# Later rectifications in the expert layers, and a re-timed first cosine layer

## The chip, the cores and the metric

The kernel runs on one core of one Trainium2 chip. The metric is the device time of the whole program in microseconds (us). The engines are TensorE (PE in the rows: matmuls; PEld: its weight loads), VectorE (DVE), ScalarE (ACT), GpSimd (POOL) and SyncE (SP, which only issues transfers). Each engine works through its own instructions in order. A wait of its oldest instruction holds up all that stand behind it.

## The reference, cut to what matters

Three stages follow each other on 1536 tokens of width 512:

```
x = attention(q, k, v)            # 2 x 8 heads, 768 positions, sinks and a window of 128
P = sinkhorn(exp(x @ w_gate))     # weights of 8 experts for each token, 8 rounds
x = sum over e of P[:, e] * (max(x @ w1[e], 0) @ w2[e])     # w1[e] 512x1024, w2[e] 1024x512
h = x @ w_in                      # 512 -> 2048
out = (h * cos(h)) @ w_out        # 2048 -> 512
```

## The kernel before, in words

**Layers.** The kernel treats the eight experts and the two halves of the last stage as ten equal layers: `e` = 0 to 7 are experts (rectified), `e` = 8 (called `E`) and `e` = 9 are the two halves of `w_in` and `w_out` (cosine). Each layer runs for the two batches `b` = 0 and 1, so there are 20 layer-batches. Each has a first part of 28 products and a second part of six output tiles.

**First part.** Every matrix is kept as a high and a low half-precision piece, and a product is six matmuls with 384 columns (high by low, low by high, high by high, for two blocks). The multiplication by `w1` uses a scheme of seven products in place of eight, so sums of products are needed. In the experts (`g1`, with the order of products in `CHAIN`), some sums are made in the accumulating bank itself: after product 0 the bank is copied out by ScalarE (line 935), and only then may product 4 add to the same bank. Other sums are made by VectorE (line 939). When a sum is complete, `act_relu` (lines 882 to 884) makes the high piece (ScalarE), the rectified value (ScalarE) and the low piece (GpSimd, called the remainder below). In the cosine layers (`g1_sums`) all sums are VectorE's (line 997), and `act_cos` makes g = h cos(h) in steps: line 892 on ScalarE, 895 on VectorE, sine and square on ScalarE (900, 901), 904 on VectorE, and the two pieces on GpSimd (906, 908).

**Second part.** `g2_mm` (line 1034) multiplies the pieces `hh` by `w2`, 24 matmuls of 512 columns for each tile of 128 tokens. In a cosine layer, matmuls of the first three tiles are woven between the products as filling.

**Order.** There is no scheduler: the order on every engine is the order in which the program issues. A clock of ticks sets it. A tick passes after each product, and 24 times in the second part; so a layer-batch has GT + HT_ = 28 + 24 = 52 ticks. `put(t0, every, steps)` hangs steps on later ticks. `late` is a list of steps that `flush` issues at the next tick. What a product's result needs (its copy, its sum) is issued one product later, behind the next product's matmuls, by `settle`.

**Weights.** `w_load` loads the next layer's weights into the one buffer `st`, finds their largest magnitude in four steps (`absmax`, line 167, one reduction of 128x1024 on VectorE each), and makes a power-of-two scale from it (`scales`). The scale needs a small matmul on TensorE (line 149) that waits for VectorE's tile `diag` (line 142). `squares` (line 170) is another way to such a bound: a sum of squares on ScalarE, used in the attention stage. `w2_split` and `w1_split` then make the pieces (ScalarE line 189, VectorE line 190). In the loop over the layers, `t2` and `t1` are the ticks for `w2` and `w1` of the next layer: (load; first magnitude step, distance; first split, distance).

**Operands of the cosine layers.** `x2` prepares the last stage's input: for each batch, six calls of `x_operand` (`xops`, three for each half c of the columns), each with three subtractions on GpSimd (lines 204 to 206, tile `T`), three operations on ScalarE, three on VectorE (line 190, tile `xs`), and one transposing transfer into `XO`. The first product of a batch needs all six.

## Time and profile before

| | us |
|---|---|
| median of 3 runs | 1372.41 (1371.7 to 1373.5) |
| the profiled execution: its time | 1374.77 |
| its span | 1373.1 |
| TensorE busy in the span | 1278.2 (93%) |
| VectorE, ScalarE, GpSimd busy | 890.7, 691.9, 640.6 |

The profiled execution is one execution, and its own time is 2.36 us above the median. Attention fills the first part up to about 180 us. The expert layers come next, each of them about 119 us long. The first cosine layer runs from 1116 to 1251 us, the second to the end.

### The profile page before, as it was taken

The numbers are of one execution on the slowest core, as the hardware profiler recorded it, in microseconds if no ns is written. First come the engines' busy times: TensorE is split into PE (matmuls) and PEld (weight loads), VectorE is DVE, ScalarE is ACT, GpSimd is POOL, SyncE is SP. The second block draws the span as 40 slices with busy tenths as digits, with TensorE's granted clock in tenths as the row PEclk, the third lists the DMA queues.
The fourth block names the chain that finished last, engine by engine and source line by source line (L and its number), as shares of the span: only waits on it lengthen the run. The fifth ranks groups of instructions, "written<-read, shape, count | busy, mean of one in ns | idle before, by whom it ended". The sixth has DMA issues, their size and how long they took to land.

```text
span 1373.1 us, 19781 instructions
## 1 busy us (share of the span) xinstructions
PE 1278.2 (93%) x7299; PEld 679.5 (49%) x7299; DVE 890.7 (65%) x1853; ACT 691.9 (50%) x1374; POOL 640.6 (47%) x782
## 2 busy tenths in 40 slices
PE   4656899999999999999999999999999898999998
PEld 3533555454555545455554545545455444454554
DVE  8986852766456653845665475475556589687774
ACT  6565754462635345264444616444371656575552
POOL 4555563521524363263426417333641748377643
PEclk8767899999999999999999999999999999999999
DMA  9798653011112310601231050132112232300001
GB/s 247 159 159 194 160 104 92 1 62 62 62 62 76 125 53 10 199 1 62 79 122 62 16 184 1 62 100 100 62 32 87 45 88 54 89 1 1 32 16 46
DMA packets 140689, 108.78 MB, mean 79 GB/s; under 512 B 100144, under 2 KB 115504, under 8 KB 140592
## 3 DMA queue, kind: packets, MB, share of 16 engines
q1 hardware_dynamic: 126512, 77.22, 21.7%
q0 software_dynamic: 7168, 25.17, 6.1%
q10 hardware_dynamic: 6912, 5.13, 1.4%
q8 instruction: 57, 0.93, 0.3%
q14 instruction: 40, 0.33, 0.1%
HBM read 71.84 MB, written 11.53 MB: 61 GB/s over the span
## 4 chain that ended last, share of the span: by engine, by line
PE 60%; ACT 11%; DVE 9%; POOL 5%; issue 2%; DMA 0%; POOLq 0%; DVEq 0%
PE bank L1034 37%; PE bank L966 19%; ACT tmp L883 4%; ACT hh L882 4%; PE bank L983 3%; DVE tmp L939 2%; DVE tmp L997 2%; ACT tmp L935 2%; DVE wm L167 1%; DVE w1o L190 1%; DVE tmp L895 1%; POOL hh L884 1%; DVE xs L190 1%; DVE tmp L904 1%; POOL S L275 1%
## 5 line engine op out<-in xcount | busy, mean ns | idle before, releaser
L1034 PE MATMUL bank<-w2s,hh 128*128 128x512 f16 x2880 | 639.4, 380 | 6.2 <-POOL hh L906 2.4
L966 PE MATMUL bank<-xo,w1o 128*128 128x384 f16 x2688 | 455.2, 328 | 21.5 <-ACT tmp L935 16.0
L1034 PEld LDWEIGHTS <-hh 128*128 128x128 f16 x2880 | 281.1, 98 | 340.6 <-POOL hh L908 4.5
L884 POOL TENSOR_TENSOR hh<-tmp,hh 128x384 f16<-128x384 f32 x256 | 230.3, 918 | 388.1 <-ACT tmp L883 376.0
L966 PEld LDWEIGHTS <-w1o 128*128 128x128 f16 x2688 | 261.3, 98 | 202.1 <-issue 34.1
L935 ACT ACTIVATE tmp<-bank 128x384 f32<-128x384 f32 x192 | 91.5, 484 | 315.6 <-PE bank L966 314.6
L939 DVE TENSOR_TENSOR tmp<-bank,tmp 128x384 f32<-128x384 f32 x192 | 103.3, 554 | 194.2 <-ACT tmp L935 166.7
L882 ACT ACTIVATE hh<-tmp 128x384 f16<-128x384 f32 x192 | 99.6, 519 | 55.1 <-DVE tmp L939 55.0
L983 PE MATMUL bank<-xo,w1o 128*128 128x384 f16 x672 | 119.4, 328 | 2.8 <-DVE tmp L997 1.2
L1098 DVE SCALAR_TENSOR_TENSOR acc<-bank,PS,acc 128x512 f32<-128x512 f32 x84 | 62.6, 746 | 69.9 <-PE bank L1034 69.8
L883 ACT ACTIVATE tmp<-tmp 128x384 f32<-128x384 f32 x192 | 100.4, 523 | 6.1
L983 PEld LDWEIGHTS <-w1o 128*128 128x128 f16 x672 | 65.9, 98 | 54.6 <-issue 7.7
L167 DVE TENSOR_REDUCE wm<-st 128x1 f32<-128x1024 f32 x72 | 86.3, 1209 | 4.9 <-DMA st<-w_in 4.9
L906 POOL TENSOR_SCALAR hh<-tmp 128x384 f16<-128x384 f32 x64 | 45.7, 714 | 90.2 <-DVE tmp L904 87.7
L189 ACT ACTIVATE w1o<-S,s 128x1024 f16<-128x1024 f32 x40 | 45.8, 1146 | 78.0 <-POOL S L276 77.3
L190 DVE SCALAR_TENSOR_TENSOR w1o<-st,s,w1o 128x512 f16<-128x512 f32 x72 | 65.9, 947 | 18.0 <-ACT w1o L189 18.0
L190 DVE SCALAR_TENSOR_TENSOR w1o<-S,s,w1o 128x1024 f16<-128x1024 f32 x40 | 55.7, 1394 | 28.9 <-ACT w1o L189 28.9
L190 DVE SCALAR_TENSOR_TENSOR w2s<-st,s,w2s 128x512 f16<-128x512 f32 x72 | 57.6, 816 | 24.3 <-ACT w2s L189 24.3
L908 POOL TENSOR_TENSOR hh<-tmp,hh 128x384 f16<-128x384 f32 x64 | 68.3, 1068 | 5.3
L997 DVE TENSOR_TENSOR tmp<-bank,tmp 128x384 f32<-128x384 f32 x112 | 59.2, 548 | 9.6 <-ACT tmp L1005 5.2
L189 ACT ACTIVATE w2s<-st,s 128x512 f16<-128x512 f32 x72 | 46.0, 708 | 22.5 <-DVE s L160 22.5
L579 POOL TENSOR_TENSOR parts<-xo,parts 128x512 f16<-128x512 f32 (+1 forms) x38 | 41.0, 1081 | 34.1 <-ACT parts L574 31.8
(185 smaller groups left out, 1301.7 us busy)
## 6 DMA issues: line engine op xcount, KB each, us to landing
st<-in_moe_w_dram SPq DMA_DIRECT2D x56, 512.0 KB, 6.0
f<-in_moe_w_in_dram POOLq DMA_DIRECT2D x16, 512.0 KB, 4.5
f<-in_moe_w_out_dram POOLq DMA_DIRECT2D x16, 512.0 KB, 4.3
w2p<-in_moe_w_dram SPq DMA_DIRECT2D x8, 512.0 KB, 4.3
w_in<-x POOLq DMA_DIRECT2D x16, 256.0 KB, 4.5
w_out<-x POOLq DMA_DIRECT2D x16, 256.0 KB, 4.3
st<-w_out SPq DMA_DIRECT2D x8, 512.0 KB, 5.3
st<-w_in SPq DMA_DIRECT2D x8, 512.0 KB, 7.0
```

The source lines that it names most:

```text
L167: nc.vector.tensor_reduce(out=dst, in_=src, axis=axis, op=ALU.max, apply_absolute_value=True)
L189: nc.scalar.activation(out=hi, in_=src, func=AF.Copy, scale=s)
L190: late.append(lambda: nc.vector.scalar_tensor_tensor(out=lo, in0=src, scalar=s, in1=hi, op0=ALU.mult, op1=ALU.subtract))
L882: nc.scalar.activation(out=hi, in_=src, func=AF.Relu)
L883: nc.scalar.activation(out=dst, in_=src, func=AF.Relu)
L884: nc.gpsimd.tensor_tensor(out=lo, in0=dst, in1=hi, op=ALU.subtract)
L935: nc.scalar.activation(out=t, in_=ps, func=AF.Copy)
L939: nc.vector.tensor_tensor(out=t, in0=ps, in1=t, op=ALU.add)
L966: nc.tensor.matmul(ps, W1O[:, j0 + c, wi, o, kk, :], XO[b][:, kk, o, xi, :], start=(n == 0 and o in (0, 5, 1)), stop=(n == 5), skip_group_ ...
L983: nc.tensor.matmul(ps, W1O[:, j, wi, o, kk, :], XO[b][:, kk, o, xi, :], start=(n == 0), stop=(n == 5))
L997: nc.vector.tensor_tensor(out=t, in0=x, in1=y, op=ALU.add)
L1034: nc.tensor.matmul(ps, HH[:, hi, f, t * 128:(t + 1) * 128], w[:, wi, f, :], start=(f == order[0] and n == 0), stop=(f == order[-1] and n = ...
```

## The change

Four edits. First, in `g1`, `out` no longer calls `act` at once: the call passes through `late` twice, so that it is issued one product later, behind what the next product's `settle` issues. (Products whose result is rectified straight from the bank, product 6, are not delayed.) Second, the six operands of batch 1 of the first cosine layer: three of them (c = 0) are hung on ticks 4, 11 and 18 of that layer's first part, the other three on ticks 37, 41 and 45, in its second part; before, all six were hung on ticks 5 to 27 of the first part. Third, at `e` = 8 the four magnitude steps of the next `w2` become `squares` on ScalarE, 5 ticks apart. Fourth, other ticks for `e` = 7 and `e` = 8.

```diff
@@ g1
             def out(c, name, ps, half, high):
                 t = q.pop((c, name))
                 nc.vector.tensor_tensor(out=t, in0=ps, in1=t, op=ALU.add)
-                act(t, (NJ if high else 0) + j0 + c, half)
+                late.append(lambda: late.append(lambda: act(t, (NJ if high else 0) + j0 + c, half)))
@@ layers
-                put(HT_ + 5 if b else HT_ + 4, 4.5 if b else 7.0, xops)
+                if b:
+                    put(HT_ + 4, 7.0, xops[:3])
+                    put(HT_ + GT + 9, 4.0, xops[3:])
+                else:
+                    put(HT_ + 4, 7.0, xops)
@@ the loop over the layers
-                ld2, ld1 = w_load(e + 1, "w2", None, st), w_load(e + 1, "w1", None, st)
+                junk = W2S[1][:, 0, 0:2].rearrange("p f w -> p (f w)").bitcast(BF16) if e == E else None
+                ld2, ld1 = w_load(e + 1, "w2", None, st, junk), w_load(e + 1, "w1", None, st)
                 t2, t1 = (3, 9, 3.0, 28, 2.25), (GT + HT_ + -16, GT + HT_ + 6, 2.5, GT + HT_ + GT + 0, 1.0)
...
                 if e == E:
-                    t2, t1 = (0, 5, 3.0, 39, 1.25), (GT + HT_ + -3, GT + HT_ + 0, 3.5, GT + HT_ + GT + 10, 0.5)
+                    t2, t1 = (0, 6, 5.0, 41, 1.4), (GT + HT_ + -1, GT + HT_ + 5, 3.0, GT + HT_ + GT + 10, 0.5)
+                if e == E - 1:
+                    t2, t1 = (3, 8, 2.5, 24, 1.25), (35, 43, 2.0, GT + HT_ + GT + 0, 1.0)
```

**On ScalarE, in an expert layer.** From the end of the first half of the products to the copies of the second half, the rows before are these (L935 copies a bank, L882 and L883 rectify; bank_80 and bank_81 are the two accumulating banks):

```order
L882 ACTIVATE hh<-bank_81 128x384
L883 ACTIVATE tmp<-bank_81 128x384
L882 ACTIVATE hh<-tmp 128x384
L883 ACTIVATE tmp<-tmp 128x384
L882 ACTIVATE hh<-tmp 128x384
L883 ACTIVATE tmp<-tmp 128x384
L882 ACTIVATE hh<-tmp 128x384
L883 ACTIVATE tmp<-tmp 128x384
L935 ACTIVATE tmp<-bank_80 128x384
L935 ACTIVATE tmp<-bank_81 128x384
```

The same place of the same layer now:

```order
L882 ACTIVATE hh<-bank_81 128x384
L883 ACTIVATE tmp<-bank_81 128x384
L882 ACTIVATE hh<-tmp 128x384
L883 ACTIVATE tmp<-tmp 128x384
L882 ACTIVATE hh<-tmp 128x384
L883 ACTIVATE tmp<-tmp 128x384
L935 ACTIVATE tmp<-bank_80 128x384
L882 ACTIVATE hh<-tmp 128x384
L883 ACTIVATE tmp<-tmp 128x384
L935 ACTIVATE tmp<-bank_81 128x384
```

The copy of bank_80 has passed one pair of rectifying operations. The same happens to the copy of bank_81 earlier in each half, which passes the pair of the sum before it. Expert 0's first batch, which is woven into the attention, keeps its order.

**On VectorE, at the start of the first cosine layer.** Before (L997 sums products, L895 and L904 belong to the cosine, L167 is a magnitude step, L190 on `xs` an operand of batch 1):

```order
L997 TENSOR_TENSOR tmp<-bank_80,tmp 128x384
L167 TENSOR_REDUCE wm<-st 128x1
L997 TENSOR_TENSOR tmp<-bank_81,tmp 128x384 x2
L190 SCALAR_TENSOR_TENSOR xs<-acc_75,s,xs 128x2x128
L190 SCALAR_TENSOR_TENSOR xs<-acc_75,s,xs 128x128
L904 SCALAR_TENSOR_TENSOR tmp<-tmp 128x384
L895 SCALAR_TENSOR_TENSOR tmp<-tmp,scl 128x384
L997 TENSOR_TENSOR tmp<-bank_84,tmp 128x384
L895 SCALAR_TENSOR_TENSOR tmp<-tmp,scl 128x384
L190 SCALAR_TENSOR_TENSOR xs<-T,s,xs 128x4x128
L167 TENSOR_REDUCE wm<-st 128x1
```

Now (line 997 has become 998):

```order
L998 TENSOR_TENSOR tmp<-bank_80,tmp 128x384
L190 SCALAR_TENSOR_TENSOR xs<-acc_75,s,xs 128x2x128
L190 SCALAR_TENSOR_TENSOR xs<-acc_75,s,xs 128x128
L998 TENSOR_TENSOR tmp<-bank_81,tmp 128x384 x2
L904 SCALAR_TENSOR_TENSOR tmp<-tmp 128x384
L895 SCALAR_TENSOR_TENSOR tmp<-tmp,scl 128x384
L998 TENSOR_TENSOR tmp<-bank_84,tmp 128x384
L190 SCALAR_TENSOR_TENSOR xs<-T,s,xs 128x4x128
L895 SCALAR_TENSOR_TENSOR tmp<-tmp,scl 128x384
```

The four reductions are gone from this part, and of the six operands three are left in it; the other three stand behind the last line 904 of the part, among the pieces of `w2`.

**On TensorE, around the scale of the next `w2`.** Before, its matmul (line 149) stood after product 17 of the 28 of the first cosine layer's batch 0, with more products behind it:

```order
L1034 LDWEIGHTS hh
L1034 MATMUL bank_85<-w2s_72,hh 128x512
L149 LDWEIGHTS one_93
L149 MATMUL bank_80<-diag,one_93 128x128
L983 LDWEIGHTS w1o
L983 MATMUL bank_81<-xo_69,w1o 128x384
```

Now it stands behind the last product of the batch (line 983 has become 984, line 1034 has become 1035):

```order
L984 LDWEIGHTS w1o
L984 MATMUL bank_78<-xo_69,w1o 128x384
L149 LDWEIGHTS one_93
L149 MATMUL bank_79<-diag,one_93 128x128
L1035 LDWEIGHTS hh
L1035 MATMUL bank_83<-w2s_72,hh 128x512
```

What follows it is the filling that is left over, and the second part.

## Rows read from the trace of the kernel before

**Rows 1.** Waits of TensorE from 278 to 1052 us: total us, times, longest
```profile
PE bank L966 <- ACT tmp L935: 8.7, 14, 1.0
PE bank L1034 <- DVE w2s L190: 1.1, 2, 0.6
```

**Rows 2.** Timeline of TensorE: start, us, instructions, idle time before with releaser
```profile
476.73 1.14 PE L966 MATMUL bank<-xo,w1o 128*128 128x384 f16 x6 [0.95 <-ACT tmp L935]
...
1072.69 1.81 PE L966 MATMUL bank<-xo,w1o 128*128 128x384 f16 x6 [3.45 <-ACT tmp L935]
...
1074.40 10.90 PE L966 MATMUL bank<-xo,w1o 128*128 128x384 f16 x60
```

**Rows 3.** Timeline of ScalarE in expert 2, batch 1, ahead of the first wait above
```profile
468.12 0.47 ACT L935 ACTIVATE tmp<-bank 128x384 f32<-128x384 f32 x1
...
475.24 0.51 ACT L882 ACTIVATE hh<-tmp 128x384 f16<-128x384 f32 x1
475.78 0.52 ACT L883 ACTIVATE tmp<-tmp 128x384 f32<-128x384 f32 x1
476.21 0.85 ACT L935 ACTIVATE tmp<-bank 128x384 f32<-128x384 f32 x2
```

**Rows 4.** Timeline of all engines in expert 7, batch 1, ahead of the second wait
```profile
1069.48 1.20 DVE L167 TENSOR_REDUCE wm<-st 128x1 f32<-128x1024 f32 x1
1069.56 0.45 POOL L206 TENSOR_TENSOR T<-acc,T 128x128 f32<-128x128 f32 x1
...
1070.58 0.71 ACT L189 ACTIVATE xs<-T,s 128x512 f16<-128x512 f32 x1
...
1072.17 0.85 ACT L935 ACTIVATE tmp<-bank 128x384 f32<-128x384 f32 x2
```

**Rows 5.** Windows: first cosine layer's batches 0, 1, second's batch 0; busy us, clock
```profile
1116.22:1191.98 75.76, 64.01 (x316) 30.94 (x315) 62.25 (x123) 45.66 (x84) 40.74 (x50) 0.95 0.35 86
1191.98:1250.97 58.99, 58.59 (x314) 30.51 (x313) 46.86 (x81) 37.37 (x67) 40.92 (x47) 1.00 0.03 13
1250.97:1310.48 59.51, 58.71 (x314) 30.45 (x312) 42.10 (x74) 30.79 (x58) 31.17 (x34) 1.00 0.06 23
```

**Rows 6.** Timeline of TensorE in the first cosine layer, batch 0
```profile
1118.02 3.57 PE L983 MATMUL bank<-xo,w1o 128*128 128x384 f16 x21 [1.14 <-DMA xo<-xs]
1122.54 0.22 PE L149 MATMUL bank<-diag,one 128*128 128x128 bf16 x1 [0.95 <-DVE diag L142]
...
1150.99 0.23 PE L149 MATMUL bank<-diag,one 128*128 128x128 bf16 x1 [4.69 <-DVE diag L142]
...
1170.29 0.61 PE L1034 MATMUL bank<-w2s,hh 128*128 128x512 f16 x2 [2.14 <-POOL hh L906]
1171.29 20.85 PE L1034 MATMUL bank<-w2s,hh 128*128 128x512 f16 x88 [0.39 <-POOL hh L908]
```

**Rows 7.** VectorE on `xs`, 1120 to 1176 us: ns min/median/max, and its idle time
```profile
L190 DVE SCALAR_TENSOR_TENSOR xs<-acc,s,xs x12: 345/542/1039, 1127.0 to 1169.8; 128x256 f16<-128x256 f32 x6, 128x128 f16<-128x128 f32 x6
L190 DVE SCALAR_TENSOR_TENSOR xs<-T,s,xs x6: 735/812/1059, 1131.1 to 1173.5; 128x512 f16<-128x512 f32 x6
...
  ACT xs L189: 2.9, 4
```

**Rows 8.** Magnitude steps on VectorE, 1120 to 1176 us: busy us, mean ns
```profile
L167 DVE TENSOR_REDUCE wm<-st 128x1 f32<-128x1024 f32 x4 | 4.8, 1208 | 0.0
```

**Rows 9.** Timeline of ScalarE at the first sine
```profile
1123.61 1.28 ACT L900 ACT_TABLE_LOAD   x1
...
1125.55 0.52 ACT L901 ACTIVATE tmp<-tmp 128x384 f32<-128x384 f32 x1
```

**Rows 10.** Line 170, sums of squares in the attention: ns min/median/max
```profile
L170 ACT ACTIVATE w1o<-tmp x4: 1039/1040/1041, 24.8 to 30.9; 128x1024 bf16<-128x1024 f32 x4
L170 ACT ACTIVATION_READ_ACCUMULATOR w1o<-tmp x4: 185/186/187, 25.7 to 31.9; 128x1 f32 x4
```

**Rows 11.** Transfers of operands, 1116 to 1192 us: us from issue to landing
```profile
xo<-xs SPq DMA_TRANSPOSE x6, 4.0
```

**Rows 12.** ScalarE takes out the fifth of six tiles, first cosine layer, batch 0
```profile
1187.00 0.69 ACT L1101 ACTIVATE acc<-bank,scl 128x512 f32<-128x512 f32 x1 [2.04 <-PE bank L1034]
```

**Rows 13.** Timeline of GpSimd and TensorE at the end of expert 2's first part, batch 1
```profile
485.30 6.29 POOL L884 TENSOR_TENSOR hh<-tmp,hh 128x384 f16<-128x384 f32 x7 [1.17 <-ACT tmp L883]
...
487.51 4.70 PE L1034 MATMUL bank<-w2s,hh 128*128 128x512 f16 x21
```

## The prediction

> **What bounds the kernel now.** I first read TensorE's busy share by stretch, then the list of what TensorE waits for, then its timeline, which puts each wait in its place. TensorE sets the pace: in the long middle of the program it is nearly always in a matmul, so only what it waits for, or what it does slowly, can be won. Between 278 and 1052 us, where the experts 1 to 7 run, its one large group of waits is 14 waits of at most 1.0 us, 8.7 us together, for the copy of a bank on line 935 [rows 1]. They recur at the same product of each layer-batch, the one that adds to bank A0 at the start of the second half of the products: 0.95 us in six of them, as at 476.73, 0.34 to 0.38 in eight. Expert 7's batch 1 has the same wait, but 3.45 us long, and after it the matmuls are slow for a while: six in 1.81 us where 476.73 shows 1.14, and 60 in 10.90 [rows 2].
>
> The second place is the first cosine layer's batch 0. It takes 75.76 us. The three other cosine batches have the same matmuls; the two that the windows show take 58.99 and 59.51 [rows 5]. So some 16.8 us are lost there. In those 75.76 us VectorE is busy for 62.25, in the next batch for 46.86 [rows 5]. The timeline shows where TensorE pays: 1.14 for the operands at the start, 0.95 and 4.69 for VectorE's `diag`, 2.14 and 0.39 for the pieces of h at the end [rows 6], and small ones between, which wait for VectorE's sums. After the last wait 88 matmuls of 512 columns take 20.85 us; at the pace of row 487.51 (4.70 for 21) they would take some 19.1 [rows 6, 13]. The reader is to see one thing in these rows: VectorE is late by several us all through this batch, and TensorE meets that lag wherever it must.
>
> **The later rectification.** Before the wait at 476.73, the copy that TensorE needs starts at 476.21, directly behind a pair of rectifying operations of 0.51 and 0.52 [rows 3]. The order now puts the copy ahead of that pair. That alone is 1.0 us earlier, enough for the 0.95 and for all shorter ones. The earlier copy, too, no longer waits behind a pair that itself waits for VectorE's sum. I take all 14 waits as gone, 8.7, and give back 0.5, because in expert 1 TensorE then reaches the pieces of `w2`, for which it waited 1.1 us already [rows 1], sooner: **8.2 us**, between 6.5 and 8.7. What is late next is the last rectified pieces of the first part. Row 485.30 shows seven remainders of 0.90 in 6.29 us; the last that the first output tile needs is the fourth, done at 488.9, and TensorE, starting at 487.51 with matmuls of some 0.22, reaches it after 21 of them, at 492.0 [rows 13]. That is 3.1 us of cover against a move of about 1.0, so I cost it at nothing; without the cover it would be 1.0 for each layer-batch. The last sum's remainder belongs to the other half of the tokens, three tiles later.
>
> **Expert 7, batch 1.** The wait costs 3.45, the slow matmuls after it 0.67 and, for the 60 in 10.90 against ten products of 1.02 (row 1118.02: 21 matmuls in 3.57), some 0.7: 4.8 together [rows 2, 6]. Two edits act here: the copy passes one pair, and the four reductions of 1.2 on VectorE, one of which starts at 1069.48 in the midst of the delay [rows 4], move into the second part of the batch before. What remains is an operand: ScalarE's operation at 1070.58 needs GpSimd's `T`, done at 1070.0, and still stands ahead of the copies [rows 4]. Without the reductions I let `T` come 1.5 us earlier (nothing would be the low end, half of four times 1.2, or 2.4, the high one). Then 1068.5, plus 0.71, a pair of 1.0 and a copy of 0.47 is 1070.7; TensorE wants it at 1072.69 - 3.45 = 1069.2. So a wait of about 1.5 stays, with 0.5 for the copy after it, and no slow matmuls: 4.8 - 2.0, **2.7 us**, between 1.0 and 4.8.
>
> **The first cosine layer, batch 0.** VectorE loses four reductions, 4.8 us [rows 8], and three of six operands: the first twelve operations have a median of 0.54 and the other six of 0.81, so 2 x 0.54 + 0.81 = 1.9 each and 5.7 for three; half of the 2.9 us idle before them goes too, 1.4 [rows 7]. Three one-column operations are added, taken at some 0.15 each, 0.5 together. In all VectorE is shorter by 4.8 + 5.7 + 1.4 - 0.5 = 11.4. ScalarE gets four sums of squares, 1.04 + 0.19 each, 4.9 us [rows 10], but the three operands leave it; it was busy for 45.66 of 75.76 [rows 5], so I cost this at nothing. Without that cover it is at most 4.9 on the chain through the cosine.
>
> A rule weighed here. The first sine is preceded by a load of tables of 1.28 us, and the square that follows it at 1125.55 has no load of its own [rows 9]. The changed order has no further load either. The Trainium skill ("ScalarE: Activation LUTs", section "Table sets: the hidden batching unit") says that functions of different sets, when alternated, cost a switch of about 2.7 us each time. By that rule alone, four squares among sines would be eight switches, an estimate of 21 us; the row shows that square and sine share a set, and the sum goes by the row.
>
> TensorE cannot win more than the batch lost: the floor is 58.99 plus the waits of 1.14 and 0.95 at the start, whose chain (GpSimd and VectorE finishing the last layer) the change leaves as it is, so 61.1 and a gain of 14.7. If VectorE stays the bound, the gain is its 11.4. The scale's matmul now stands behind the last product, so TensorE meets VectorE's lag once there. I take **11.0**, nearer to VectorE's figure because the batch was VectorE's; low end 7, if the lag at that matmul is still as large as the 4.69 of before and is not covered.
>
> **Costs behind it.** The three late operands end close to batch 1. The last is begun behind the removal of the fourth tile, one tile of 5.2 us (24 matmuls at 0.22) before row 1187.00 [rows 12]; three operations on ScalarE, two pieces of `w2` and VectorE's part take about 4 us, the transfer 4.0 [rows 11], and about 10.4 us are left to TensorE: cover of some 2 us. Every us beyond it is paid by TensorE at the first product. The load of the next `w1` follows the later splits. I set **1.0 us** for all this, 0 to 3.
>
> **Sum.** 8.2 + 2.7 + 11.0 - 1.0 = 20.9. The profiled execution's own time is 1374.77, so it would be 1353.9; it is 2.4 above the median of 1372.41, and against the median the forecast is **1351.5 us**. With the ends of all terms: gains of 28.2 to 11.5, so 1344.2 to 1360.9. A difference of 0.2%, some 2.7 us, is about what a measurement of this kernel can tell from no change.
>
> **Rivals.**
> 1. VectorE's lag stays and is paid at the scale's matmul. For it: TensorE has paid 4.69 at the same kind of matmul. Against: 11.4 us of VectorE's work have left. With a gain of 5 there and 3 of costs behind it, 8.2 + 2.7 + 5 - 3 = 12.9 less: 1359.5. Chance 0.14.
> 2. The batch clears fully: 8.7 + 4.8 + 14.7 = 28.2, 1344.2. For it: batch 1 with four reductions in it has almost no waits (58.59 busy of 58.99 [rows 5]). Against: three operands and the late start of VectorE remain. Chance 0.13.
> 3. The waits for copies only move, to the remainders or to other copies: the 8.2 falls away, 1359.7. Against it stand 3.1 us of cover. Chance 0.08.
> 4. Slower: the rectified pieces come so late that TensorE waits at the start of the second part in all 14 layer-batches of experts 1 to 7. It pays from 3.1 us of delay on, and outweighs the gain from 3.1 + 20.9 / 14 = 4.6 us on; at 5 us it is 14 x 1.9 = 26.6, so 1378. The order moves the pieces by one pair, 1.0. Chance 0.04.
> 5. The added squares bring table loads after all: eight of 1.28 are 10.2 us on ScalarE, 1361.7 if all are paid. Chance 0.01.
> The forecast itself, within 1346 to 1357, has 0.57, and 0.03 is left for a time within 0.2% of before. Faster 0.93, same 0.03, slower 0.04. The range of 1344 to 1361 takes in the first three rivals and both ends of the terms.
>
> **What the new profile would show.** TensorE's waits for line 935 in the experts near zero, and no new ones for the remainders of line 884. In expert 7's batch 1 a wait under 2 us, without slow matmuls behind it. The first cosine layer's batch 0 at about 65 us, the wait for `diag` at its end under 3 us. At the start of batch 1 a wait for `xo` under 1 us. The forecast is wrong if TensorE waits for the operands of batch 1, if VectorE's busy time in batch 0 stays above 55 us, or if copies still reach ScalarE behind work that waits.

## The result, and the profile after

| | before | after |
|---|---|---|
| median, us | 1372.95 (4 runs) | 1355.68 (4 runs, 1354.42 to 1357.88) |
| ratio, 95% interval | | 0.9877 (0.986 to 0.9894) |
| the profiled execution: time, span | 1374.77, 1373.1 | 1356.48, 1354.8 |

The gain is 17.3 us by the medians and 18.3 by the two profiled executions. The forecast was 20.9, and the time lies inside the range. The parts of the sum did not come out as forecast: two errors of opposite sign made the total look better than its working, and that the total came so near is luck in part.

I read the new trace by stage, from the start of one layer-batch on TensorE's timeline to the start of the next. The last stage ends with TensorE's last matmul, 4.0 us before the end of the span in both traces:

| stretch | before | after | forecast of the change |
|---|---|---|---|
| start to expert 1 (attention, expert 0) | 278.70 | 280.53 | none |
| experts 1 to 7 | 837.52 | 821.18 | -10.9 |
| first cosine layer, batch 0 | 75.76 | 69.55 | -11.0 |
| first cosine layer, batch 1 | 58.99 | 61.41 | +1.0 |
| second cosine layer, both batches | 118.05 | 118.06 | none |

The experts gave 16.3 us, half as much again as forecast. The first cosine layer gave 3.8 where I had 10.0. Expert 0 took back 1.6.

**The experts.** The list of TensorE's waits between 280.53 and 1041.31 us, the stretch of [rows 1], has one row left:

```profile
PE bank L1035 <- DVE w2s L190: 0.2, 1, 0.2
```

All 14 waits for line 935 (8.7 us) are gone, and the waits for pieces of `w2`, which I had expected to grow, have nearly gone too. ScalarE's timeline at the place of [rows 3] shows the copy with one pair behind it that stood in front of it before. It starts 14.8 us after the start of the batch in place of 17.2, the copy at 474.27 already waits for TensorE, and TensorE's row (the last one here) runs through without a wait:

```profile
471.34 0.49 ACT L935 ACTIVATE tmp<-bank 128x384 f32<-128x384 f32 x1
471.73 0.51 ACT L882 ACTIVATE hh<-tmp 128x384 f16<-128x384 f32 x1
472.27 0.52 ACT L883 ACTIVATE tmp<-tmp 128x384 f32<-128x384 f32 x1
472.70 0.47 ACT L935 ACTIVATE tmp<-bank 128x384 f32<-128x384 f32 x1
474.27 0.49 ACT L935 ACTIVATE tmp<-bank 128x384 f32<-128x384 f32 x1 [1.09 <-PE bank L967]
...
456.51 17.71 PE L967 MATMUL bank<-xo,w1o 128*128 128x384 f16 x108
```

In expert 7's batch 1 the timeline of TensorE answers to the second and third row of [rows 2]: a wait of 1.38 where 3.45 stood, and 60 matmuls in 9.91 where they took 10.90.

```profile
1059.54 1.14 PE L967 MATMUL bank<-xo,w1o 128*128 128x384 f16 x6 [1.38 <-ACT tmp L935]
1060.88 9.91 PE L967 MATMUL bank<-xo,w1o 128*128 128x384 f16 x60 [0.21 <-ACT tmp L935]
```

The later rectification costs something in one place, expert 0's batch 1, where the gating of the experts shares GpSimd. Eight remainders run there back to back behind a reduction of the gating (line 647). Counted from the start of the batch, that reduction starts at 25.7 us in place of 25.2 and the remainders at 33.5 in place of 32.4, long after ScalarE has done the first of their pieces (26.8 and 25.8). The waits of TensorE for them (214.74 to 280.53 us) are three times as large as before, 2.2 in place of 0.7:

```profile
PE bank L1035 <- POOL hh L884: 2.2, 2, 1.2
```

**The first cosine layer.** The windows that answer to [rows 5] (length; busy us of TensorE, weight loads, VectorE, ScalarE, GpSimd; granted clock):

```profile
1101.71:1171.26 69.55, 62.05 (x315) 31.05 (x314) 58.76 (x121) 49.36 (x92) 38.86 (x50) 0.95 0.32 74
1171.26:1232.67 61.41, 58.82 (x314) 30.34 (x313) 48.78 (x81) 37.54 (x67) 41.00 (x47) 1.00 0.11 35
```

VectorE's busy time fell by only 3.5 in a batch that became 6.2 shorter, and ScalarE's rose by 3.7. TensorE's timeline answers to [rows 6]:

```profile
1103.40 3.57 PE L984 MATMUL bank<-xo,w1o 128*128 128x384 f16 x21 [1.04 <-DMA xo<-xs]
1107.93 0.22 PE L149 MATMUL bank<-diag,one 128*128 128x128 bf16 x1 [0.96 <-DVE diag L142]
...
1118.48 1.14 PE L984 MATMUL bank<-xo,w1o 128*128 128x384 f16 x6 [1.12 <-ACT tmp L1006]
...
1141.53 3.08 PE L984 MATMUL bank<-xo,w1o 128*128 128x384 f16 x12 [2.25 <-ACT tmp L1006]
...
1146.54 0.26 PE L149 MATMUL bank<-diag,one 128*128 128x128 bf16 x1 [1.93 <-DVE diag L142]
1146.60 24.83 PE L1035 MATMUL bank<-w2s,hh 128*128 128x512 f16 x108
...
1197.69 0.23 PE L149 MATMUL bank<-diag,one 128*128 128x128 bf16 x1 [2.52 <-DVE diag L142]
```

The wait for `diag` fell from 4.69 to 1.93 and the waits for the pieces of h at the end went. Two new ones came, 1.12 and 2.25, for ScalarE's copy of a first product (line 1006). The last row is in batch 1 and new as well: the scale of the next `w1` meets a lag of 2.52, where that matmul waited 0.40 before. The operands of batch 1, for which I had set the 1.0, arrive just in time: the last one lands 0.39 us after the start of the batch, behind three matmuls that do not need it.

### The profile page after: what moved, and what is told of

The parts are those of the page before. It is cut to its first block, busy times and chain, and to the rows that moved or that the text cites. A ratio compares the mean times of both kernels' runs of the same rounds, so it can differ in the third digit from the quotient of the medians.

```text
span 1354.8 us, 19792 instructions
## 1 busy us (share of the span) xinstructions
PE 1272.4 (94%) x7299; PEld 679.7 (50%) x7299; DVE 894.3 (66%) x1852; ACT 692.4 (51%) x1382; POOL 641.1 (47%) x782
## 4 chain that ended last, share of the span: by engine, by line
PE 70%; DVE 5%; POOL 5%; issue 3%; ACT 3%; DMA 0%; POOLq 0%; DVEq 0%
PE bank L1035 38%; PE bank L967 28%; PE bank L984 4%; DVE tmp L998 1%; POOL hh L884 1%; POOL S L275 1%; DVE w1o L190 1%; DVE tmp L904 1%; POOL S L274 1%; POOL S L276 1%; DVE tmp L895 1%; ACT tmp L900 1%; POOL S L273 0%; ACT tmp L901 0%; POOL hh L908 0%
## 5 line engine op out<-in xcount | busy, mean ns | idle before, releaser
L935 ACT ACTIVATE tmp<-bank 128x384 f32<-128x384 f32 x192 | 93.4, 487 | 339.8 <-PE bank L967 338.7
L882 ACT ACTIVATE hh<-tmp 128x384 f16<-128x384 f32 x192 | 98.9, 515 | 13.2 <-DVE tmp L939 13.2
L883 ACT ACTIVATE tmp<-tmp 128x384 f32<-128x384 f32 x192 | 100.4, 523 | 6.1
L906 POOL TENSOR_SCALAR hh<-tmp 128x384 f16<-128x384 f32 x64 | 45.9, 717 | 84.0 <-DVE tmp L904 84.0
L167 DVE TENSOR_REDUCE wm<-st 128x1 f32<-128x1024 f32 x68 | 81.5, 1208 | 0.0
L190 DVE SCALAR_TENSOR_TENSOR w1o<-st,s,w1o 128x512 f16<-128x512 f32 x72 | 64.9, 934 | 15.2 <-ACT w1o L189 15.2
L190 DVE SCALAR_TENSOR_TENSOR w1o<-S,s,w1o 128x1024 f16<-128x1024 f32 x40 | 55.2, 1380 | 20.4 <-ACT w1o L189 20.4
L190 DVE SCALAR_TENSOR_TENSOR w2s<-st,s,w2s 128x512 f16<-128x512 f32 x72 | 56.4, 797 | 10.3 <-ACT w2s L189 10.1
```

What stands on the lines that cost most here:

```text
L167: nc.vector.tensor_reduce(out=dst, in_=src, axis=axis, op=ALU.max, apply_absolute_value=True)
L190: late.append(lambda: nc.vector.scalar_tensor_tensor(out=lo, in0=src, scalar=s, in1=hi, op0=ALU.mult, op1=ALU.subtract))
L882: nc.scalar.activation(out=hi, in_=src, func=AF.Relu)
L883: nc.scalar.activation(out=dst, in_=src, func=AF.Relu)
L935: nc.scalar.activation(out=t, in_=ps, func=AF.Copy)
```

## The experiments

The times of one kernel differ by up to 7 us from run to run, and part of that comes from the attention: TensorE's first product of expert 0 stands at 101.50 us in e2's profile and at 106.30 in e1's. From there on the expert stretch repeats well (821.17 to 821.25 in the twelve profiles with the later rectification), so the verdicts go by stages first. The first cosine layer repeats less well: the changed kernel, e2 and e11 have the same instructions in the same order there, and their batch 0 takes 69.55, 68.30 and 69.91, their batch 1 61.41, 62.79 and 62.70. A difference of 1.3 us in one batch is therefore no difference by itself. Expert stretch, first cosine layer's batch 0 and batch 1, second cosine layer, in us. (In e4, e10 and e11 the second cosine layer starts without the wait of 0.4 to 0.5 us for a first copy that the others have.)

| kernel | median | ratio (interval) | experts 1-7 | batch 0 | batch 1 | second |
|---|---|---|---|---|---|---|
| before | 1373 | 1 | 837.52 | 75.76 | 58.99 | 118.05 |
| after | 1355.68 | 0.9877 (0.986-0.9894) | 821.18 | 69.55 | 61.41 | 118.06 |
| e1 late only | 1357.42 | 0.9886 (0.9871-0.9901) | 821.25 | 75.46 | 59.00 | 118.06 |
| e2 no late | 1370.56 | 0.998 (0.9971-0.9989) | 837.49 | 68.30 | 62.79 | 118.06 |
| e3 magnitudes on VectorE | 1356.23 | 0.9875 (0.9862-0.9889) | 821.20 | 69.39 | 62.80 | 118.07 |
| e4 six operands | 1361.00 | 0.9908 (0.9894-0.9921) | 821.19 | 75.79 | 62.85 | 117.53 |
| e5 late and half | 1356.45 | 0.9879 (0.9865-0.9892) | 821.23 | 68.84 | 64.12 | 118.06 |
| e6 w1 places | 1354.81 | 0.9871 (0.9854-0.9888) | 821.18 | 69.73 | 60.83 | 118.06 |
| e7 sine later | 1362.02 | 0.9927 (0.9914-0.9941) | 821.17 | 71.89 | 62.16 | 123.02 |
| e8 all three | 1366.19 | 0.9952 (0.994-0.9965) | 821.25 | 69.25 | 68.01 | 123.27 |
| e9 copy first | 1352.58 | 0.9848 (0.9829-0.9867) | 821.19 | 69.50 | 59.15 | 118.07 |
| e10 scales later | 1361.29 | 0.9914 (0.9897-0.9931) | 821.18 | 72.99 | 67.59 | 116.92 |
| e11 expert 0 as before | 1354.57 | 0.9861 (0.9842-0.988) | 821.19 | 69.91 | 62.70 | 117.40 |
| e12 copy first, scale later | 1351.23 | 0.9843 (0.9825-0.9861) | 821.19 | 68.73 | 59.01 | 118.07 |

**e1: the later rectification alone.** The kernel before, with one edit:

```diff
-                act(t, (NJ if high else 0) + j0 + c, half)
+                late.append(lambda: late.append(lambda: act(t, (NJ if high else 0) + j0 + c, half)))
```

> Kernel before, with only the later rectification. Theory (the later rectification is worth more than the 8.2 us that I gave it, since it clears the 3.45 us wait of expert 7's batch 1 too): the 14 waits on line 935 go (8.7 us), expert 1 gives 1.1, the 3.45 falls below 1.5, expert 0's batch 1 costs 1.5 to 2.2; 10 to 12 us faster than before, some 1361 to 1363, and the first cosine layer's batch 0 stays near 75 us. Rival (the reductions moved out of expert 7 did the rest): the 3.45 stays at 2.5 or more, 7 to 8.5 us faster, 1364.5 to 1366.

More than either expected: 15.8 us by the medians, and 16.27 in experts 1 to 7, the same as the whole change. Expert 7's batch 1 is 60.36 us long, though its four reductions stand where they stood. Its wait is that of the whole change:

```profile
1060.34 1.14 PE L967 MATMUL bank<-xo,w1o 128*128 128x384 f16 x6 [1.39 <-ACT tmp L935]
```

The cosine layers did not move.

**e2: everything but the later rectification.** The edit is e1's, taken out of the changed kernel.

> The changed kernel without the later rectification (the other edits alone). Theory: the 14 waits on line 935 return, 8.7, with expert 1's 1.1 and part of expert 7's, and expert 0's 2.2 goes; 9 to 11 us slower than the changed kernel, 1365 to 1367, with the first cosine layer's batch 0 at 69 to 70 us. Rival (the two parts help each other, the first cosine layer starts cleaner behind the later rectification): that layer's batch 0 is 72 us or more and the time 1368 or more.

2.6 us faster than before, 14.9 slower than the changed kernel. The expert stretch is back at 837.49. The reductions that were moved out of expert 7 give 0.6 there without the later rectification (63.21 for 63.82) and nothing with it. Batch 0 of the first cosine layer is not worse for the missing edit, 68.30, so the rival falls: the two parts do not help each other. The profile shows more, since from the first cosine layer on this kernel has the instructions and the order of the changed one. The scale's matmul starts 44.9 us after the start of the batch, as in the changed kernel (44.8), but the 108 matmuls behind it take 23.47 in place of 24.83, and in batch 1 TensorE then waits 1.25 for the late operands:

```profile
1158.75 0.22 PE L149 MATMUL bank<-diag,one 128*128 128x128 bf16 x1 [1.32 <-DVE diag L142]
1158.81 23.47 PE L1034 MATMUL bank<-w2s,hh 128*128 128x512 f16 x108
...
1184.01 10.40 PE L983 MATMUL bank<-xo,w1o 128*128 128x384 f16 x63 [1.25 <-DMA xo<-xs]
```

The last operand lands 70.1 us after the start of batch 0 here, and 69.9 us in the changed kernel. Its arrival holds both: what batch 0 wins is waited for at the start of batch 1.

**e3 and e4: which of the two edits made batch 0 shorter.** e3 gives the magnitude steps back to VectorE at their new places (its condition never holds), e4 hangs all six operands on the first part again:

```diff
# e3
-                junk = W2S[1][:, 0, 0:2].rearrange("p f w -> p (f w)").bitcast(BF16) if e == E else None
+                junk = W2S[1][:, 0, 0:2].rearrange("p f w -> p (f w)").bitcast(BF16) if e > 99 else None
# e4
-                if b:
-                    put(HT_ + 4, 7.0, xops[:3])
-                    put(HT_ + GT + 9, 4.0, xops[3:])
-                else:
-                    put(HT_ + 4, 7.0, xops)
+                put(HT_ + 5 if b else HT_ + 4, 4.5 if b else 7.0, xops)
```

> The changed kernel with the magnitudes of the next w2 taken on VectorE again (four reductions of 1.2 us, at the new places), nothing else. Theory A (in the first cosine layer's batch 0 ScalarE's squares hold the copies of line 1006): the two waits of 1.12 and 2.25 us for these copies go, VectorE pays part of 4.8; between 2 us faster and 1 us slower than the changed kernel. Theory B (VectorE is still the bound there, as I forecast): 3 to 5 us slower, 1359 to 1361, with the loss at the scale's matmul and at VectorE's sums.

> The changed kernel with all six operands of batch 1 back in the first part of the first cosine layer's batch 0 (places and pace of before). Theory B (VectorE is the bound): VectorE has 7.1 us more to do there and the batch takes 4 to 7 us longer, 1360 to 1363. Theory A (ScalarE is the bound): three operands are some 3 us of ScalarE's work too, so 2 to 4 us longer, 1357.5 to 1360, with longer waits for line 1006. If neither, within 1 us.

With e1 and the changed kernel these two make a square of four (the ticks of the next `w2` differ too between e1 and the others). The windows of batch 0, in order: e1 (six operands, magnitudes on VectorE), e4 (six, on ScalarE), e3 (three, on VectorE); the changed kernel's (three, on ScalarE) stands above.

```profile
1102.51:1177.97 75.46, 63.51 (x315) 30.92 (x314) 62.72 (x123) 45.62 (x84) 40.48 (x50) 0.95 0.35 86
```
```profile
1099.47:1175.26 75.79, 62.79 (x315) 30.94 (x314) 56.86 (x121) 49.52 (x92) 40.18 (x50) 0.95 0.30 70
```
```profile
1098.08:1167.47 69.39, 61.62 (x316) 30.77 (x314) 61.96 (x118) 45.65 (x84) 38.93 (x50) 0.98 0.32 71
```

The batches as a whole hardly tell reductions from squares: 75.46 and 75.79 with six operands, 69.39 and 69.55 with three. The three operands are worth 6.1 and 6.2. But the end of a batch hides something. Behind the scale's matmul TensorE runs 108 matmuls without a wait, and these took 23.47 in e3, 24.83 in the changed kernel and 25.83 in e4:

```profile
1144.11 0.22 PE L149 MATMUL bank<-diag,one 128*128 128x128 bf16 x1 [1.07 <-DVE diag L142]
1144.16 23.47 PE L1035 MATMUL bank<-w2s,hh 128*128 128x512 f16 x108
```
```profile
1149.54 0.26 PE L149 MATMUL bank<-diag,one 128*128 128x128 bf16 x1 [5.40 <-DVE diag L142]
1149.60 25.83 PE L1035 MATMUL bank<-w2s,hh 128*128 128x512 f16 x108
```

So I also read where VectorE ends the last step of the cosine in batch 0 (line 904), how long it was busy until then, and where the scale's matmul starts, in us from the start of the batch:

| kernel: operands in the first part, magnitudes on | last step of line 904 ends | VectorE busy until then | scale's matmul |
|---|---|---|---|
| e1: six, VectorE | 59.18 | 55.25 | (earlier in the order) |
| e4: six, ScalarE | 58.27 | 50.71 | 50.07 |
| e3: three, VectorE | 52.66 | 49.65 | 46.03 |
| changed: three, ScalarE | 51.46 | 45.92 | 44.83 |
| e2: the same here | 51.57 | 46.04 | 44.93 |

The squares take 4.5 and 3.7 us off VectorE, and its last step ends only 0.9 and 1.2 us earlier. The rest has become waits: VectorE's idle time until then, nearly all of it for ScalarE, rises from 3.9 to 7.6 and from 3.0 to 5.5. The three operands, which need both engines, take 5.6 and 4.8 off VectorE and end its last step 6.5 and 6.8 earlier. So VectorE with the reductions is close to being the bound (busy for 94% of the time in e3), and without them the chain through both engines is. My theory B had the direction; it expected 3 to 5 us where 1.2 are found. Theory A had one half: in e3, without squares, the wait of 1.12 for line 1006 is gone, but the later one is there and 2.76 long. Its ScalarE shows why; the copy of 0.47 stands behind a pair of sine and square that waited for VectorE's reduction of the angle (line 895):

```profile
1137.69 0.61 ACT L900 ACTIVATE tmp<-tmp,scl 128x384 f32<-128x384 f32 x1 [0.91 <-DVE tmp L895]
1138.34 0.52 ACT L901 ACTIVATE tmp<-tmp 128x384 f32<-128x384 f32 x1
1138.77 0.47 ACT L1006 ACTIVATE tmp<-bank 128x384 f32<-128x384 f32 x1
1139.14 0.60 ACT L900 ACTIVATE tmp<-tmp,scl 128x384 f32<-128x384 f32 x1
```

**e5 and e6: where batch 1's loss comes from.** e5 is the kernel before with the later rectification and e4's edit the other way round, nothing else. e6 is the changed kernel with one table entry of before:

```diff
# e6
-                    t2, t1 = (0, 6, 5.0, 41, 1.4), (GT + HT_ + -1, GT + HT_ + 5, 3.0, GT + HT_ + GT + 10, 0.5)
+                    t2, t1 = (0, 6, 5.0, 41, 1.4), (GT + HT_ + -3, GT + HT_ + 0, 3.5, GT + HT_ + GT + 10, 0.5)
```

> Kernel before with two of the edits, the later rectification and half of the operands in the next part; magnitudes on VectorE and all places of the w1 and w2 steps as before. Theory (the half of the operands is worth all that the first cosine layer's batch 0 won, and the new places of w1 cost the 2.4 us of its batch 1): batch 0 at 69 to 70 us, batch 1 at 59 to 60, so 1 to 2.5 us faster than the changed kernel, 1353 to 1354.7. Rival (the new places are what lets the late operands through): batch 1 stays at 61 us or more or batch 0 rises above 71, 1356 to 1358.

> The changed kernel with the places of the second cosine layer's w1 steps as before (magnitudes from 0 with pace 3.5 in place of 5 with pace 3.0, loads two ticks earlier). Theory (the scale's matmul stands where VectorE lags by 2.5 us): its wait in batch 1 falls from 2.52 to about 0.4 us, batch 1 from 61.4 to about 59, 1353.3. Rival (the late operands make VectorE lag there whatever the place): a wait of 2 us or more stays, or comes as a wait for operands, and the time is within 1 us of the changed kernel.

In e5 the rival was right: batch 1 takes 64.12, and its first products wait for the late operands, the cost that I had feared:

```profile
1172.13 11.79 PE L984 MATMUL bank<-xo,w1o 128*128 128x384 f16 x63 [2.76 <-DMA xo<-xs]
...
1193.89 0.22 PE L149 MATMUL bank<-diag,one 128*128 128x128 bf16 x1 [1.21 <-DVE diag L142]
```

The landing of the last operand, counted from the start of batch 0, shows what the other edits do for it: 72.1 us in e5, 71.2 in e3, which has the new places and magnitudes on VectorE, and 69.9 to 70.1 with the squares (changed kernel, e2, e11). So the new places and the squares each bring the operands about 1 us forward. e3 waits 1.25 for them, and e2, with the squares, waits 1.25 too because its batch 0 was that much shorter; the changed kernel waits for none because its batch 0 ended later.

At the scale of `w1` in batch 1 two things meet. e4, which has the new places but no late operands, waits 2.55 there, and e3 2.54; e5, with late operands and the places of before, waits 1.21; e1, with neither, 0.40. e6 shortens that wait from 2.52 to 1.45 and batch 1 to 60.83, between its theory (0.4) and its rival (2 or more); its time cannot be told from the changed kernel's.

**e7 and e8: the first edit's idea in the cosine.** The sine and its square go one product later, in the changed kernel (e7) and in e5 (e8):

```diff
-            for d, f in zip((1, 1, 3), (red, sine, fin)):
+            for d, f in zip((1, 2, 3), (red, sine, fin)):
```

> The changed kernel with the sine and its square issued one product later, in all four cosine batches. Theory (a copy of line 1006 stands on ScalarE behind sine and square, and these wait for VectorE's reduction): the waits of 1.12 and 2.25 us go, the first cosine layer's batch 0 falls from 69.5 to 65 to 67 us, 2 to 4 us faster, 1352 to 1353.5. Rival (the pieces of h come a product too late): waits for lines 906 and 908 of about 1 us at the end of each of the four batches, 1357 to 1360.

> The later rectification, half of the operands in the next part, and the sine a product later; magnitudes and places as before. If both theories hold, batch 0 of the first cosine layer at 65 to 67 us and batch 1 at 59 to 60: 1350 to 1352. If only one of them holds, 1353 to 1355; if none, 1357 or more.

A miss, 6.3 us slower than the changed kernel. The largest wait for line 1006 hardly moves (1.99), and the three batches behind batch 0 now end with waits for the pieces of h. In the second cosine layer's first batch, which had none at its end:

```profile
1275.10 1.69 PE L1035 MATMUL bank<-w2s,hh 128*128 128x512 f16 x7 [0.79 <-POOL hh L908]
1277.07 0.60 PE L1035 MATMUL bank<-w2s,hh 128*128 128x512 f16 x2 [0.28 <-POOL hh L906]
1278.24 17.22 PE L1035 MATMUL bank<-w2s,hh 128*128 128x512 f16 x79 [0.57 <-POOL hh L908]
```

The experts had cover for a later rectification and the cosine has none. e8 adds e5's late operands (a wait of 2.74) to that.

**e9: the copy first.** The opposite remedy on the changed kernel: leave the pair, and issue the copy of a first product ahead of it.

```diff
                 settle()
-                pend.append((None, lambda: use(ps)))
+                if o == 0:
+                    use(ps)
+                else:
+                    pend.append((None, lambda: use(ps)))
                 tick()
```

> The changed kernel with the copy of a first product in the cosine layers (line 1006) issued right behind its own product, ahead of the pairs of sine and square that the order set before it. Theory (these copies are held by one pair each, 1.1 us, and by what the pair waits for): the waits of 1.12 and 2.25 us shrink to nothing and to 1 us or less, the first cosine layer's batch 0 goes from 69.5 to 66.5 to 68 us, 1353 to 1354.5. Rival (VectorE's lag is only met a few us later): the wait at the scale's matmul grows by as much, and the time stays within 1 us.

Both were right, one in each batch. In batch 0 the waits for line 1006 shrink to 0.21, and the wait at the scale grows from 1.93 to 4.14: the scale's matmul starts 44.5 us after the start of the batch in place of 44.8, so VectorE's lag is met a few us later, and the batch stays at 69.50. In batch 1 the wait of 2.52 at the scale is gone and the batch is back at 59.15. TensorE's timeline in batch 0 (the edit has moved line 1006 to 1009, 998 to 1001):

```profile
1137.49 1.14 PE L984 MATMUL bank<-xo,w1o 128*128 128x384 f16 x6 [0.21 <-ACT tmp L1009]
1138.99 1.14 PE L984 MATMUL bank<-xo,w1o 128*128 128x384 f16 x6 [0.37 <-DVE tmp L1001]
1144.27 0.22 PE L149 MATMUL bank<-diag,one 128*128 128x128 bf16 x1 [4.14 <-DVE diag L142]
```

**e10: the scales later.** The changed kernel with its magnitude steps spread wider, so that scale and matmul come later:

```diff
-                    t2, t1 = (0, 6, 5.0, 41, 1.4), (GT + HT_ + -1, GT + HT_ + 5, 3.0, GT + HT_ + GT + 10, 0.5)
+                    t2, t1 = (0, 6, 7.0, 41, 1.4), (GT + HT_ + -1, GT + HT_ + 6, 6.0, GT + HT_ + GT + 10, 0.5)
```

> The changed kernel with the magnitudes of the second cosine layer's weights spread wider, so that both scales' matmuls stand 7 and 13 ticks later, behind the last product, where TensorE needs nothing of VectorE. Theory (1.93 and 2.52 us are paid only because the matmul of line 149 stands where VectorE lags): both waits fall under 0.5, batch 1 back to 59 us, batch 0 to 67 to 68; 3 to 4.5 us faster, 1351 to 1352.7. Rival (the lag stays and is met at the pieces of h): new waits for lines 906 and 908 and less than 1.5 us won.

A miss: the waits are 3.88 and 6.26, longer than before the move. VectorE's timeline ahead of the first shows the reason. The steps of the scale now stand behind further steps of the cosine (line 904), and the last of these wait for ScalarE:

```profile
1147.16 0.56 DVE L904 SCALAR_TENSOR_TENSOR tmp<-tmp 128x384 f32<-128x384 f32 x1 [0.44 <-ACT tmp L901]
1148.22 0.68 DVE L904 SCALAR_TENSOR_TENSOR tmp<-tmp 128x384 f32<-128x384 f32 x1 [0.50 <-ACT tmp L901]
1148.82 0.14 DVE L253 TENSOR_REDUCE wmm<-wm 128x1 f32<-128x4 f32 x1
...
1149.94 0.37 DVE L142 TENSOR_SCALAR diag<-eye,p 128x128 bf16<-128x128 bf16 x1
```

**e11: expert 0 as before.** The changed kernel, with the rectification of expert 0 issued at once (`act` called directly when e is 0).

> The changed kernel with the later rectification for experts 1 to 7 alone; expert 0 keeps the order of before. Theory (in expert 0's batch 1 the later pieces of h cost the two waits of 1.24 and 0.93 us): that batch is 0.5 to 1.2 us shorter, 64.6 us, and the time 1354.5 to 1355.2, hardly apart from the changed kernel's. Rival (GpSimd holds these pieces anyway): no difference in that batch.

TensorE's waits for these remainders fall from 2.2 to 1.0 and expert 0's batch 1 from 65.79 to 64.99. That is the size expected, and too small for the medians to show. The comparison flatters it: the other profiles with the later rectification have 65.06 to 65.80 there, and the two without it (before, e2) 64.64 and 64.59. So the later order costs this batch 0.4 to 1.2 us, and the rival has a share: before, after and in e11 alike these remainders start only 7.2 to 7.8 us behind the start of the reduction on line 647, long after the first of their pieces is done.

**e12: the copy first, and the scale's matmul alone later.** e9, with the matmul issued later and VectorE's steps left alone:

```diff
-        late.append(product)
+        def wait(n):
+            late.append(product if n == 0 else lambda: wait(n - 1))
+        wait({f"w2{E + 1}": 9, f"w1{E + 1}": 4}.get(tag, 0))
```

> The kernel with the copy first, and the matmul of the two scales of the second cosine layer (line 149) alone issued later: the one for w2 nine ticks, 27 matmuls, the one for w1 four; VectorE's steps stay where they are. Theory (VectorE's lag at the end of the products is real, and only part of it is paid at the scale): the wait of 4.14 us falls under 0.5 and 1.5 to 3 us of it come back at the pieces of h (lines 906 and 908), so 1 to 2.5 us faster than with the copy first alone, 1350 to 1351.5. Rival (all of the lag comes back there): 1352 to 1353.5.

TensorE's timeline at the end of batch 0's products (lines 906 and 908 are 909 and 911 here):

```profile
1144.38 0.61 PE L1041 MATMUL bank<-w2s,hh 128*128 128x512 f16 x2 [2.55 <-POOL hh L909]
1145.77 3.17 PE L1041 MATMUL bank<-w2s,hh 128*128 128x512 f16 x7 [0.79 <-POOL hh L911]
1148.73 0.30 PE L149 MATMUL bank<-diag,one 128*128 128x128 bf16 x1
```

The matmul of line 149 waits for nothing any more, and 3.3 of the 4.14 us come back at the pieces of h: batch 0 gains 0.8. The time lies in the theory's range, but of the two expectations the rival was the nearer in the mechanism. With 1351.23 this is the fastest kernel of the study. Its interval still overlaps that of the change (0.9825 to 0.9861 against 0.986 to 0.9894); the two batches of the first cosine layer, 127.74 for 130.96, put it 3.2 us ahead.

## Why the prediction was right in total, and where its parts were wrong

**The later rectification: right mechanism, a term too small.** I had 8.2 for it and 2.7 for expert 7. e1 shows that this one edit gives 16.3 by itself. Two parts of that were mis-sized, and one was credited to the wrong edit.
- In the twelve batches between expert 1's batch 1 and expert 7's batch 0, 711.46 us became 701.78: 9.7 gained for listed waits of 7.4 (8.7 less the 0.95 and 0.34 of expert 1's batch 0). In the profile a wait costs more than its idle time, since the products on either side of it no longer overlap: after a wait six matmuls take 1.14, inside a run they add 0.97 (108 in 17.71, 102 in 16.74). Twelve times 0.17 is 2.0, most of the difference.
- In expert 1's batch 0 I gave back 0.5 "because in expert 1 TensorE then reaches the pieces of `w2` ... sooner". The sign was wrong. The batch gained 3.24: the pieces of `w2` are made on the same ScalarE, and their last operation there ends 29.8 us after the batch's start in place of 33.6.
- In expert 7's batch 1 the remaining wait was forecast well (1.5, measured 1.38; the batch gained 3.4 for 2.7), but the 1.5 credited to the moved reductions belongs to the later rectification. ScalarE's operation on `T` starts 16.1 us after the batch's start with the later rectification and 18.2 before; in e1, without the moved reductions, it is 16.1 too.

The cover for the remainders held everywhere but in expert 0, which the sum did not look at: its batch 1 pays 0.4 to 1.2. (Both its batches together took 1.6 more in this profile, but batch 0, which is woven into the attention, differs by more than that between profiles.)

**The first cosine layer: the step that failed.** It is the term of 11.0: in it 11.4 us less work of VectorE were taken as 11.4 us less time, and ScalarE's squares were costed "at nothing" because it was busy for 45.66 of 75.76. VectorE's last step of the cosine in batch 0 ended 59.3 us after the start of the batch before and ends at 51.5 now, 7.8 earlier. The operands did what the sum said, 6.5 to 6.8 for 7.1. The reductions did not: 4.3 were set for them (4.8 less 0.5), and 0.9 to 1.2 came. Every cosine passes from VectorE to ScalarE, back to VectorE, to ScalarE and back again, in two queues that work in order, so a step that is moved from one queue to the other stays in the way; some 3 of the 4.9 that I gave as the bound for a ScalarE without cover were paid, as waits of VectorE for ScalarE. Of the 7.8, TensorE's batch kept 6.2 in the changed kernel and 7.5 in e2; the difference is the pace of the 108 matmuls behind the scale's. That the low end of 7 is near to this is luck: it was meant for a wait of 4.69 at the scale's matmul, and the wait was 1.93.

Two of the three signs that I had set for a wrong forecast came. Copies (line 1006) still reach ScalarE behind work that waits, and VectorE's busy time in batch 0 is 58.76, above 55. The second sign was badly set: three operands have moved only into the second part of the same batch, so the window still holds them, while up to the last step of the cosine VectorE's busy time fell from 55.3 to 45.9. The third, a wait of TensorE for the operands of batch 1, stayed away by little (the landing 0.39 us into the batch) and came in e2.

**The costs behind it: the size was short and the place another.** 1.0 was set for late operands, with a cover of some 2 us. That cover is used up: in the changed kernel they just arrive, in e2 and e3 TensorE waits 1.25 and in e5 2.76. In the changed kernel the price is 2.4 at another spot, the scale of `w1` in batch 1, which stands worse at its new place (2.55 even in e4, without late operands). e9 shows that this wait hangs on the copies as well: with the copy ahead of the pair it is gone.

**The rivals.** Rival 1 had the cosine nearly right, a gain of 5 there and 3 behind it (measured 6.2 and 2.4), and TensorE did pay 1.93 at the scale's matmul. It missed the time by 3.8, most of all because it kept the 8.2 and the 2.7. Rival 2, a batch that clears fully, needed 61.1 us in batch 0, and no kernel came below 68.3. Rivals 3 and 4 did not come: no wait for remainders appears in experts 1 to 7. Nor did rival 5: ScalarE still loads its tables once in the cosine layers.

Batch 0 still takes 9.7 us longer than batch 1 in the best kernel. Waits of 7.0 us are listed there (operands 1.06, scale 0.96, pieces of h 4.4, copies and sums 0.6), 1.5 is in slow matmuls behind the last of them (7 in 3.17), and the 0.17 beyond the idle time of each of these eight waits would account for the rest. What stays open is what would remove them. The chain of the first operands, GpSimd and VectorE at the end of the last expert, was not tried, and a shorter batch 0 would now meet the late operands (a wait of 0.34 in this kernel).

## What to carry to other kernels

On an engine that works in order, an operation that waits for another engine holds everything behind it; set the short copies that TensorE needs ahead of such operations, as long as what is set back has cover, which is to be read for each stage by itself. Where two engines hand a value to and fro, a busy time that is taken off one is not yet time won: 3.7 to 4.5 us moved from VectorE to ScalarE ended the chain 0.9 to 1.2 us earlier, while three operands taken away from both ended it 6.5 to 6.8 earlier. Compare such edits at the place where the chain ends, and not only by the whole stage, whose rest can run at another pace. When a wait is moved away, ask what the same lag, or the next late arrival, meets next, and count a wait as its idle time plus the overlap that it breaks.

## What the runs showed of the hardware that was not expected

The same instructions after the same wait run slowly in one execution and not in another. The slow ones stand where the granted clock is at the lower of its two levels, 1.2 in place of 2.4 GHz. In the changed kernel 12 matmuls took 3.08 us after the wait of 2.25 in batch 0; in e11, after the same 2.25, 12 took 2.11. Behind the scale's matmul the 108 matmuls took 24.83 in the changed kernel, where the pace of 144 in 31.24 would give 23.4, 25.14 in e11 and 23.47 in e2. In batch 1 the six matmuls behind the scale's took 1.14 in the changed kernel after a wait of 2.52, and 2.13 in e11 after 2.55. The windows show the clock (the number behind the five busy times): 0.50 at the start of the 108 in the changed kernel, 1.00 over nearly all of them in e2, where the lower level fell on the 12 before (3.69 for 12, after the wait of 2.25).

```profile
1146.60:1149.00 2.40, 2.40 (x7) 0.88 (x7) 2.40 (x6) 1.18 (x2) 0.88 (x2) 0.50 0.00 0
```
```profile
1158.80:1182.10 23.30, 23.30 (x109) 10.53 (x109) 18.08 (x32) 16.62 (x30) 11.76 (x17) 1.00 0.32 50
```

In all these cases TensorE had waited shortly before. What decides on which matmuls the lower level falls was not tried. In front of the scale's matmul the slow 12 cost no time here, since that matmul starts 44.8 to 44.9 us after the start of the batch in the changed kernel, e2 and e11 alike; behind it the slow matmuls lengthen the batch.
